# Two FNet-plus-attention layers on one core: the P·V sum's PSUM bank exchanged with the bank of the maxima, and six steps instead of eight between a tile's row maxima and its scores

## The chip, the core and the metric

The program runs on one NeuronCore of a Trainium2 chip. It uses the engines TensorE (PE in the profile; its weight loads stand apart as PEld), VectorE (DVE), ScalarE (ACT), GpSimd (POOL), and the queue engine SyncE (SP), which issues DMAs. The metric is the device time of one execution in microseconds. The kernel before took 3445.49 us in the median of three runs (3443.53 to 3445.89).

## What is computed

Two layers, one after the other. Each mixes x by a real Fourier transform over hidden size and sequence, and then adds multi-query attention with 32 heads of size 16 and one shared K and V:

```python
x = x + Re(DFT_seq(DFT_hidden(layernorm(x))))          # x: 2048 x 512
q = (layernorm(x) @ wq) -> 32 heads x 2048 x 16;  k, v = layernorm(x) @ wk, @ wv   # 2048 x 16 each
p = softmax(q @ k.T / 4)                                # 32 x 2048 x 2048
x = x + concat_heads(p @ v) @ wo
...                                                     # the same two again
```

## The kernel before

Each layer has a phase a (the two transforms, layer norm, K, V and Q, and some row maxima) and a phase b (the attention and the output projection). The change touches phase b alone, which the function `phase_b` writes out step by step.

Phase b walks over 16 tiles of 128 queries (index i), and each tile over 32 steps (s_); n = 32 i + s_ counts them through. A step takes half of the heads (hf 0 in steps 0 to 15, hf 1 in 16 to 31) against one chunk of 128 keys, and contains:

- **four scores** (`score`, L1119): K against four query pairs, 512 columns each, into a PSUM bank; ACT then takes the exponential of each bank into SBUF (L1121). Four banks `o.x` go round for this.
- **three maxima** of a later tile (`whole` with `max_of`, L450 and L451, and `part`, L1070 to L1075): query against 512 keys into a bank, and DVE reduces the bank to its maximum. `part` does two halves of 256 keys in one bank, with a one-element copy on DVE (L1072) between them. Three banks `o.banks` go round: a maximum takes the first of the list, and the bank goes to the end of the list.
- **the P·V matmuls** (`pv`, L1133) of the step two steps earlier, four matmuls in fp32 (eight records in the trace), summed over 16 steps into one bank "z". At the sum's end (pv of steps 15 and 31, so issued in steps 17 and 1) the bank is copied to SBUF, by ACT (L1144) or by DVE (L1142), and the next sum begins in the same bank one step later.

Step 17 also holds the output projection of the tile before (`o_proj`, 12 matmuls at L102 to L104 into one of the maxima's banks `po`, and ACT's copy of it, L1207).

How many maxima a step gets is decided by `share(n)`: three, or two where n % 32 == 1 and the maxima are at least SPARE (3) ahead of their due times. A step with two maxima gives the sum's end to DVE instead of ACT. The due times (`goals`) lie AHEAD steps before the end of a tile or half. When no maxima are left, n_max is 0, and the kernel changes to "wide" steps: exponentials of 1024 columns (L1114), in other banks.

The maxima of a tile reach its scores in this way, all of it placed by AHEAD = 8 (`at` is 24 for a whole tile): in steps at - 1 and at DVE reduces the partial maxima (`max_neg_a`, L594), in step at + 1 POOL splits them into a high and a low part (`max_neg_b`, L603 and L604), and in step at + 2 DVE transposes them (`max_rows`, L609) and 16 DMAs (L615), eight issued by SP and eight by POOL, write them into the rows 48, 49 and 112, 113 of the tile's queries `qT`. The first scores of the tile, in its step 0, read these rows. For tile 0's second half and for the halves of the tiles 14 and 15, the same goes on with half as many pairs, and for the second halves with `at` = 8.

Each engine works through its own list of instructions in order; a wait for a semaphore holds up everything behind it on that engine. The order in the lists is the order in which the code is written.

Of the kernel before, what the change touches and what calls it, by code (L numbers as in the profile page):

```python
# [22 lines left out]
NT = S // P  # L23
NK = D // P
TB = 4
NPAIR = H // 2
# [1 line left out]
KR = 64  # L28
M0 = 48
NSTEP = 32  # L30
AHEAD = 8
SPARE = 3


# [10 lines left out]
HALF = NPAIR // 2  # L45
# [3 lines left out]
def fnet_mqa_kernel(ctx: ExitStack, tc: tile.TileContext, x_in, ct, dt_, wq, wkv, wo, out):  # L49
    nc = tc.nc  # L50
# [160 lines left out]
    def make_layer(L, src, mid, dst, last):  # L211
        o = Layer()
# [232 lines left out]
            return o.mxp[i]  # L445

        def max_of(i, pr, g, c0, n, to):
            pm = (o.banks.pop(0) if o.banks else bank("y"))[:, :n]
            gs = slice(64 * g, 64 * g + KR)
            nc.tensor.matmul(pm, o.qT[i][gs, pr, :], kz[gs, c0:c0 + n], start=True, stop=True)  # L450
            nc.vector.reduce_max(to, pm, axis=AX.X)  # L451
            if o.banks:
                o.banks.append(pm)

        def max_two(pr, g, c0, to):
            pm = bank("y")
# [575 lines left out]
        ahead, parts = [], []  # L1032
# [62 lines left out]
        def done_with(i, pr):  # L1095
            return all(u[:2] > (i, pr) for u in todo + parts + ahead)

        ptiles = {}
        wide = []
# [26 lines left out]
        def pv(i, s_, n_max=3):  # L1126
            hf, c = divmod(s_, NT)
            if c == 0:
                acc[i, hf] = bank("z")
            a = acc[i, hf]  # L1130
            pt = ptiles.pop((i, s_))
            for j in range(4):
                nc.tensor.matmul(a[32 * j:32 * j + 32, :], v1[:, c, :], pt[:, j, :], start=c == 0, stop=c == NT - 1)  # L1133
            if c == NT - 1:
                oa = half(hf)
                if last and (i, hf) == (NT - 1, 1):
                    ob = half(0)[:, :256]
                    nc.scalar.copy(oa[:, :256], a[:, :256])
                    nc.vector.tensor_copy(ob, a[:, 256:])
                    oa = (oa, ob)  # L1140
                elif wide and hf == 0 or n_max == 2:
                    nc.vector.tensor_copy(oa, a)  # L1142
                else:
                    nc.scalar.copy(oa, a)  # L1144
                acc[i, hf] = oa
# [41 lines left out]
            nc.gpsimd.tensor_copy(bt["oh"][:, cs], bt["ot"][:, cs])  # L1187
            nc.gpsimd.tensor_sub(bt["ol"][:, cs], bt["ot"][:, cs], f(bt["oh"][:, cs]))

        def o_mm(k):  # L1190
            if k == 0:
                bt["po"] = o.banks.pop(0) if o.banks else bank("y")
            ks = slice(k * P, (k + 1) * P)
            mm3(bt["po"], bt["oh"][:, ks], bt["ol"][:, ks], woh[:, k, :], wol[:, k, :], k == 0, k == NK - 1)

# [2 lines left out]

        def o_proj(i):
            for k in range(NK):  # L1200
                o_mm(k)
            o_add(i)

        def o_add(i):
            if o.banks or wide:
                raw = half(3)
                nc.scalar.copy(raw, bt["po"])  # L1207
                o.banks.append(bt["po"])
                nc.gpsimd.tensor_add(bt["x"], raw, bt["x"])
            else:  # L1210
                nc.vector.tensor_add(bt["x"], bt["po"], bt["x"])
            (nc.sync if last else nc.gpsimd).dma_start(dst[i], bt["x"])
# [82 lines left out]
        def phase_b(nxt):  # L1295
            nonlocal woh, wol, osp
            o.x = pair() + pair()
            o.banks = [bank("y") for _ in range(3)]
            woh = slot(4, F32R).rearrange("p (k e) -> p k e", k=NK)
            wol = slot(5, F32R).rearrange("p (k e) -> p k e", k=NK)  # L1300
            def wo_load(j):
                st["wo", j] = half(4 + j)
                nc.sync.dma_start(st["wo", j], wo[:, j, :])

            behind = []
            for n in range(NT * NSTEP):
                i, s_ = divmod(n, NSTEP)
                n_max = share(n) if todo or parts or ahead else 0
                if len(behind) == 2:
                    pv(*behind.pop(0), n_max)  # L1310
                behind.append((i, s_))
                out_now = i > 0 and s_ == NT + 1
                if out_now:
                    o_proj(i - 1)
                if out_now and n_max == 3:
                    o.x.append(o.banks.pop())
                    o.banks.append(o.x.pop(0))
                if n_max == 0 and not wide:
                    banks_as(f"wide{L}")
                    o.banks = [bank("v")]  # L1320
                    wide.extend(bank("w") for _ in range(3))
                at = part_next() if n_max == 3 else None
                if at:
                    for k, v in zip("asMssMsb", (0, 1, 0, 3, 0, 1, 2, 1)):
                        if k == "s":
                            score(i, s_, v)
                        elif k == "M":
                            whole(v)
                        else:
                            part(at, v)  # L1330
                else:
                    g = side()
                    turns = ((g, 0), (1 - g, min(n_max, 2)), (2 + g, 0), (3 - g, n_max - 2))
                    if out_now and n_max == 2:
                        whole(g)
                        turns = ((1 - g, 0), (g, 1), (3 - g, 0), (2 + g, 0))
                    for j, m in turns:
                        score(i, s_, j)
                        for _ in range(m):
                            more_max()  # L1340
                if n in (1, 3):
                    q_half_store(12, 2 + n // 2)
                if i == 0 and 17 <= s_ <= 23 and s_ % 2:
                    q_half_store(14, s_ // 2 - 8)
                if 12 <= n < 16:
                    wo_load(n - 12)
                if n == 25:
                    osp = slot(3, F32R).rearrange("p (a h n) -> p a h n", a=2, h=2)
                if i == 0 and s_ in (16, 18, 20, 22):
                    j = s_ // 2 - 8  # L1350
                    nc.gpsimd.tensor_copy(woh[:, j, :], st["wo", j])
                    nc.gpsimd.tensor_sub(wol[:, j, :], st["wo", j], f(woh[:, j, :]))
                if i > 0:
                    for fn in out_tasks(i - 1).get(s_, ()):
                        fn()
                for j in range(2, NT):
                    if i == (j // 4 if j < 5 else j - 4 if j < 13 else j - 2):
                        at = {2: 0, 3: 12, 4: 6}.get(j, 0)
                        if s_ == at:
                            qT_load(j)  # L1360
                        if s_ == at + 4:
                            o.loaded.add(j)
                for fn in half_tasks(i).get(s_, ()):
                    fn()
                for at, j, p0, np_ in ((NT - AHEAD, i, HALF, HALF), (NSTEP - AHEAD, i + 1, 0, HALF if i >= NT - 3 else NPAIR)):
                    if j in (0, NT - 2, NT - 1) or j == i + 1 < NT:
                        for e in range(2):
                            if s_ == at - 1 + e:
                                assert done_with(j, p0 + np_ // 2 * (e + 1) - 1)
                                max_neg_a(j, p0, np_, parts=(e,))  # L1370
                        if s_ == at + 1:
                            max_neg_b(np_, nc.gpsimd)
                        if s_ == at + 2:
                            max_rows(j, p0, np_)
            if nxt is not None:
                wide.clear()
                banks_as(f"single{L + 1}")
                nxt.a_start()
            for at in behind:
                pv(*at)  # L1380
            if nxt is not None:
                o.banks = []
            return {**out_tasks(NT - 1), 12: [lambda: o_proj(NT - 1)]}
# [67 lines left out]
```

## Time and profile before

| | |
|---|---|
| median of three runs | 3445.49 us |
| the profiled execution's own time | 3445.71 us |
| its span, first to last instruction | 3443.9 us |
| what lies around the span | 1.8 us |
| granted TensorE clock | 0.999 |
| phase b of layer 0, first to last exponential | 621.9 to 1724.4 us |
| phase b of layer 1 | 2331.9 to 3433.9 us |
| one step of phase b | about 2.1 us |
| one wide step | about 1.85 us |

The busy time of PE comes from modelled ends of pipelined matmuls, so 99% does not mean that PE is at its peak. Groups of instructions carry the line that recorded them, so L1133 is every P·V matmul.

### The profile page before, as it was taken

What the parts mean: (1) busy time and instruction counts of PE and PEld (TensorE: products, weight loads), DVE (VectorE), ACT (ScalarE), POOL (GpSimd) and SP (SyncE); (2) the same over time, 40 slices, a digit from 0 to 9 for tenths busy, and PEclk for the clock granted to TensorE, in tenths of its full rate; (3) what the DMA queues carried; (4) which work ended last, traced back from release to release, by engine and by line L of the source; (5) the groups of instructions that cost most, each with busy time, mean ns of one, the idle gap of its engine ahead of it and who ended that gap; (6) DMA issues with size and microseconds to landing.
All of it is one profiled execution on the core that took longest, in us unless ns stands there. A gap on an engine that the chain in (4) does not pass through costs nothing.

```text
span 3443.9 us, 68599 instructions
## 1 busy us (share of the span) xinstructions
PE 3415.1 (99%) x25532; PEld 2016.1 (59%) x25532; DVE 2664.0 (77%) x5792; ACT 2665.6 (77%) x5228; POOL 936.9 (27%) x1478
## 2 busy tenths in 40 slices
PE   8999999999999999999999999999999999999999
PEld 6888979544444444444378989894444444444443
DVE  6264766899999999999432747669989998999893
ACT  4234644899999999999932256549999999999998
POOL 4255453312222222222313354522111111111111
PEclk9999999999999999999999999999999999999999
DMA  6445252321111100111143352523111111011110
GB/s 189 149 157 190 75 169 81 88 65 34 39 36 51 36 27 24 51 36 27 42 141 116 127 171 102 153 72 91 48 39 36 51 36 39 23 37 38 33 29 26
DMA packets 225554, 255.88 MB, mean 74 GB/s; under 512 B 52896, under 2 KB 175040, under 8 KB 218052
## 3 DMA queue, kind: packets, MB, share of 16 engines
q1 hardware_dynamic: 210932, 234.04, 21.8%
q0 software_dynamic: 14144, 17.33, 1.6%
q8 instruction: 201, 3.29, 0.4%
q14 instruction: 133, 1.09, 0.1%
q10 hardware_dynamic: 144, 0.13, 0.0%
HBM read 187.69 MB, written 65.79 MB: 74 GB/s over the span
## 4 chain that ended last, share of the span: by engine, by line
PE 92%; issue 3%; DVE 2%; ACT 2%; POOL 1%; DMA 1%; SPq 0%; DVEq 0%; ACTq 0%; POOLq 0%
PE z L1133 30%; PE x L893 11%; PE x L1119 7%; PE x L1070 6%; PE y L1119 5%; PE x L450 5%; PE y L1070 4%; PE y L450 3%; PE y L541 3%; PE x L102 3%; PE x L104 3%; PE x L103 2%; PE y L102 2%; PE y L103 2%; PE y L104 2%
## 5 line engine op out<-in xcount | busy, mean ns | idle before, releaser
L1121 ACT ACTIVATE slot<-x 128x512 f32<-128x512 f32 x2212 | 1189.0, 604 | 17.4 <-PE x L1119 2.6
L1133 PE MATMUL z<-slot,v 128*32 128x512 f32 x8192 | 1102.1, 605 | 0.8
L1121 ACT ACTIVATE slot<-y 128x512 f32<-128x512 f32 x1692 | 927.8, 606 | 8.6
L451 DVE TENSOR_REDUCE mxp<-x 128x1 f32<-128x512 f32 x1126 | 739.7, 685 | 29.7
L451 DVE TENSOR_REDUCE mxp<-y 128x1 f32<-128x512 f32 x830 | 549.2, 685 | 26.2 <-PE y L450 2.8
L1119 PE MATMUL x<-slot,kz 64*128 64x512 f32 x1662 | 516.1, 423 | 0.7 <-DMA slot<-craw 0.7
L1119 PE MATMUL y<-slot,kz 64*128 64x512 f32 x1218 | 415.3, 430 | 0.0
L1075 DVE TENSOR_REDUCE mxp<-x 128x2 f32<-128x512 f32 x556 | 378.8, 681 | 1.0 <-PE y L1119 1.0
L1070 PEld LDWEIGHTS x<-kz,slot 64*128 64x128 f32 x844 | 154.8, 183 | 348.9 <-DVE mxp L451 342.1
L893 PE MATMUL x<-cl,xnh 64*128 64x512 f32 (+1 forms) x1536 | 358.6, 354 | 0.0
L893 PE MATMUL x<-ch,xnl 64*128 64x512 f32 (+1 forms) x1536 | 346.4, 358 | 3.3 <-ACT xnl L652 3.3
L893 PE MATMUL x<-ch,xnh 64*128 64x512 f32 (+1 forms) x1536 | 346.9, 358 | 0.2
L450 PE MATMUL x<-kz,slot 64*128 64x512 f32 x858 | 343.9, 415 | 0.0
L1133 PEld LDWEIGHTS z<-slot,v 128*32 128x32 f32 x8192 | 167.1, 108 | 229.4 <-issue 184.4
L1070 PE MATMUL x<-kz,slot 64*128 64x256 f32 x844 | 280.2, 332 | 0.0
L1075 DVE TENSOR_REDUCE mxp<-y 128x2 f32<-128x512 f32 x400 | 272.5, 681 | 0.0
L1119 PEld LDWEIGHTS x<-slot,kz 64*128 64x128 f32 x1662 | 262.3, 185 | 13.6 <-ACT slot L1121 7.8
L1070 PEld LDWEIGHTS y<-kz,slot 64*128 64x128 f32 x564 | 103.7, 184 | 233.1 <-DVE mxp L451 219.8
L450 PE MATMUL y<-kz,slot 64*128 64x512 f32 x582 | 236.6, 418 | 0.6 <-DVE mxp L451 0.4
L893 PEld LDWEIGHTS x<-ch,xnh 64*128 64x128 f32 x1536 | 215.3, 184 | 17.2 <-issue 5.2
L893 PEld LDWEIGHTS x<-ch,xnl 64*128 64x128 f32 x1536 | 213.3, 184 | 19.8 <-issue 6.1
L893 PEld LDWEIGHTS x<-cl,xnh 64*128 64x128 f32 x1536 | 217.1, 185 | 8.9
(270 smaller groups left out, 6792.5 us busy)
## 6 DMA issues: line engine op xcount, KB each, us to landing
craw<-ct_in SPq DMA_DIRECT2D x112, 512.0 KB
slot<-qd SPq DMA_DIRECT2D x44, 1024.0 KB
qd<-row SPq DMA_DIRECT2D x144, 128.0 KB
od<-row SPq DMA_DIRECT2D x252, 64.0 KB
row<-wqd SPq DMA_DIRECT2D x48, 256.0 KB
row<-x_in SPq DMA_DIRECT2D x32, 256.0 KB
mid<-row POOLq DMA_DIRECT2D x32, 256.0 KB, 2.4
craw<-ct_in SPq DMA_DIRECT2D x32, 256.0 KB
```

Of the source, the lines that this page charges most:

```text
L102: nc.tensor.matmul(ps_, ah, bh, start=start, stop=False)
L103: nc.tensor.matmul(ps_, ah, bl, start=False, stop=False)
L104: nc.tensor.matmul(ps_, al, bh, start=False, stop=stop)
L450: nc.tensor.matmul(pm, o.qT[i][gs, pr, :], kz[gs, c0:c0 + n], start=True, stop=True)
L451: nc.vector.reduce_max(to, pm, axis=AX.X)
L541: nc.tensor.matmul(pm, o.qT[i][gs, pr, :], k[gs, c0:c0 + 512], start=True, stop=True)
L893: nc.tensor.matmul(z[d], a[gs, s, d * P:(d + 1) * P], b[gs, :], start=first and q < 2 and e == 0, stop=last and q > 1 and e == len(turns) - 1)
L1070: nc.tensor.matmul(pm[:, 256 * g:256 * g + 256], o.qT[i][gs, pr, :], kz[gs, c0:c0 + 256], start=True, stop=True)
L1075: nc.vector.reduce_max(partial(i)[:, pr, :, k], pm.rearrange("p (a n) -> p a n", a=2), axis=AX.X)
L1119: nc.tensor.matmul(e, kz[64 * g:64 * g + KR, c * P:(c + 1) * P], o.qT[i][64 * g:64 * g + KR, cp:cp + 4, :], start=True, stop=True)
L1121: nc.scalar.activation(ptiles[i, s_][:, j, :], e, AF.Exp, scale=DH ** -0.5)
L1133: nc.tensor.matmul(a[32 * j:32 * j + 32, :], v1[:, c, :], pt[:, j, :], start=c == 0, stop=c == NT - 1)
```

## The change

AHEAD goes from 8 to 6. `share(n)`, `left` and `goals` are as they were, so the later due times let the steps n = 353, 385, 417, 449 and 481 of each layer have two maxima as well: 15 such steps in a layer, where there were ten (33, 65, ... 321). The five sums that end there are copied by DVE instead of ACT. The five maxima that these steps leave out come later, and the first wide step is n = 489, where it was 488.

The P·V sums get a named bank `o.z`. Where DVE copies a sum's end (tiles 0 to 13), the next sum begins in the bank that a maximum has used last, and the copied bank goes to the end of the maxima's list. After an output projection, the next sum takes the projection's bank, and the sum's old bank goes to the maxima. The earlier exchange in step 17, of the projection's bank with a bank of the scores, is gone. Around tiles 14 and 15 the rules bring the sum back into its first bank before the wide steps.

The block with the maxima's last steps (L1365 to L1374) now stands ahead of the output tasks, the loads of queries and the half tasks of a step, instead of behind them.

```diff
-AHEAD = 8
+AHEAD = 6
...
         def max_of(i, pr, g, c0, n, to):
-            pm = (o.banks.pop(0) if o.banks else bank("y"))[:, :n]
+            b = o.banks.pop(0) if o.banks else bank("y")
+            pm = b[:, :n]
...
             if o.banks:
-                o.banks.append(pm)
+                o.banks.append(b)
...
         def pv(i, s_, n_max=3):
             hf, c = divmod(s_, NT)
             if c == 0:
-                acc[i, hf] = bank("z")
+                acc[i, hf] = o.z
...
                 elif wide and hf == 0 or n_max == 2:
                     nc.vector.tensor_copy(oa, a)
+                    if not wide and i < NT - 2:
+                        o.z = o.banks.pop()
+                        o.banks.append(a)
                 else:
                     nc.scalar.copy(oa, a)
...
-        def o_mm(k):
+        def o_mm(k, i=0):
             if k == 0:
-                bt["po"] = o.banks.pop(0) if o.banks else bank("y")
+                bt["po"] = o.banks.pop(next((k for k, b in enumerate(o.banks) if i == NT - 2 and b is o.zb), 0)) if o.banks else bank("y")
...
         def o_add(i):
             if o.banks or wide:
                 raw = half(3)
                 nc.scalar.copy(raw, bt["po"])
-                o.banks.append(bt["po"])
+                if not wide and o.z is not bt["po"] and (i < NT - 3 or bt["po"] is o.zb):
+                    o.banks.append(o.z)
+                    o.z = bt["po"]
+                else:
+                    o.banks.append(bt["po"])
...
             o.banks = [bank("y") for _ in range(3)]
+            o.z = o.zb = bank("z")
...
                 if out_now:
                     o_proj(i - 1)
-                if out_now and n_max == 3:
-                    o.x.append(o.banks.pop())
-                    o.banks.append(o.x.pop(0))
...
+                for at, j, p0, np_ in ((NT - AHEAD, i, HALF, HALF), (NSTEP - AHEAD, i + 1, 0, HALF if i >= NT - 3 else NPAIR)):
+                    ...
+                        if s_ == at + 1:
+                            max_neg_b(np_, nc.gpsimd)
+                        if s_ == at + 2:
+                            max_rows(j, p0, np_)
                 if i > 0:
                     for fn in out_tasks(i - 1).get(s_, ()):
                         fn()
...
                 for fn in half_tasks(i).get(s_, ()):
                     fn()
-                for at, j, p0, np_ in ((NT - AHEAD, i, HALF, HALF), ...
```

**DVE, near the end of tile 5 of layer 0.** The rows are DVE's list before; `nm` and `ms` are the maxima on their way, `mxp` the partial maxima of later tiles, and each L1075 is the last maximum of a step. The transposition L609 stands in step 26, one step ahead of the layer norm's L1268 in step 27.

```order
L1258 BN_AGGR mv<-mt 128x2
L1072 COPY x<-x 1x1
L451 TENSOR_REDUCE mxp_10992<-x 128x1
L451 TENSOR_REDUCE mxp_10992<-y 128x1
L1075 TENSOR_REDUCE mxp_10992<-x 128x2
L609 STREAM_TRANSPOSE mt<-ms 128x64
L1072 COPY x<-x 1x1
L451 TENSOR_REDUCE mxp_11905<-y 128x1
L451 TENSOR_REDUCE mxp_11905<-x 128x1
L1075 TENSOR_REDUCE mxp_11905<-x 128x2
L1268 TENSOR_SCALAR lnv<-mv 128x1
L1269 TENSOR_SCALAR lnw<-lnv 128x1
```

The same list of the changed kernel, whose lines are numbered a little higher (L610 is the transposition, L1076 a step's last maximum, L1276 and L1277 the layer norm's).

```order
L595 TENSOR_REDUCE nm<-mxp_9817 128x16
L1073 COPY y<-y 1x1
L452 TENSOR_REDUCE mxp_11896<-y 128x1 x2
L1076 TENSOR_REDUCE mxp_11896<-y 128x2
L1276 TENSOR_SCALAR lnv<-mv 128x1
L1277 TENSOR_SCALAR lnw<-lnv 128x1
L1073 COPY y<-y 1x1
L452 TENSOR_REDUCE mxp_11896<-y 128x1 x2
L1076 TENSOR_REDUCE mxp_11896<-y 128x2
L610 STREAM_TRANSPOSE mt<-ms 128x64
L1279 TENSOR_SCALAR rs<-lnw 128x1
```

The transposition has moved behind two more steps' maxima, into step 28.

**POOL, near the end of tile 3 of layer 0.** Before, POOL splits the maxima, issues its eight DMAs, and then scales the attention output of the first half (L1181 to L1188):

```order
L603 CAST ms<-nm 128x2x16
L604 TENSOR_TENSOR ms<-nm,ms 128x2x16
L615 DMA xnl<-mt 1x16x32 x8
L440 MEMSET mxp_10992 128x32x2
L1181 TENSOR_TENSOR row_10887<-row_10887,row_10888 128x256
L1187 CAST slot_8594<-row_10887 128x256
L1188 TENSOR_TENSOR slot_8594<-row_10887,slot_8594 128x256
L1273 TENSOR_TENSOR lnw<-rs 128x1
```

In the changed kernel (L1185 to L1192 scale, L616 are the DMAs, L1281 begins the layer norm's short operations):

```order
L604 CAST ms<-nm 128x2x16
L605 TENSOR_TENSOR ms<-nm,ms 128x2x16
L1185 TENSOR_TENSOR row_10880<-row_10880,row_10881 128x256
L1191 CAST slot_8590<-row_10880 128x256
L1192 TENSOR_TENSOR slot_8590<-row_10880,slot_8590 128x256
L616 DMA xnl<-mt 1x16x32 x8
L1281 TENSOR_TENSOR lnw<-rs 128x1
```

The three scaling operations have come between the split and the eight DMAs.

**PE, from the end of step 0 to step 2 of tile 4**, with the semaphores that each waits for. Before, the new sum's first P·V matmul (step 2) goes into the bank that DVE copies in step 1, and waits for DVE; the maximum behind it waits for nothing:

```order
L1133 MATMUL z<-slot_11096,v_75 32x512 x4
L1119 MATMUL x<-xnl,kz 128x512 [waits Activation_49]
L1119 MATMUL y<-xnl,kz 128x512 [waits Activation_49]
L450 MATMUL x<-kz,slot_10345 128x512 [waits DVE_49] x2
L1119 MATMUL y<-xnl,kz 128x512 [waits Activation_49] x2
L1133 MATMUL z<-slot_11118,v_75 32x512 [waits DVE_49]
L1133 MATMUL z<-slot_11118,v_75 32x512 x3
L1070 MATMUL x<-kz,slot_10345 128x256
```

In the changed kernel (L1134 is P·V, L1120 a score, L451 and L1071 maxima):

```order
L1134 MATMUL z<-slot_11089,v_75 32x512 x4
L1120 MATMUL x<-xnl,kz 128x512 [waits Activation_49] x2
L451 MATMUL y<-kz,slot_10340 128x512 [waits DVE_49] x2
L1120 MATMUL x<-xnl,kz 128x512 [waits Activation_49] x2
L1134 MATMUL y<-slot_11111,v_75 32x512 [waits DVE_49]
L1134 MATMUL y<-slot_11111,v_75 32x512 x3
L1071 MATMUL z<-kz,slot_10340 128x256 [waits DVE_49]
```

The new sum goes into a bank y, and its wait for DVE is for the last maximum of step 0, which stands ahead of the copy in DVE's list; the wait for the copy of z is now that of the maximum behind the P·V matmuls.

More of the change, by code (lines that the diff above doesn't have):

```diff
@@ L1200, in o_proj @@
             for k in range(NK):
-                o_mm(k)
+                o_mm(k, i + 1)
             o_add(i)
@@ L1314, in phase_b @@
                     o_proj(i - 1)
-                if out_now and n_max == 3:
-                    o.x.append(o.banks.pop())
-                    o.banks.append(o.x.pop(0))
                 if n_max == 0 and not wide:
+                    assert o.z is o.zb
                     banks_as(f"wide{L}")
@@ L1352, in phase_b @@
                     nc.gpsimd.tensor_sub(wol[:, j, :], st["wo", j], f(woh[:, j, :]))
+                for at, j, p0, np_ in ((NT - AHEAD, i, HALF, HALF), (NSTEP - AHEAD, i + 1, 0, HALF if i >= NT - 3 else NPAIR)):
+                    if j in (0, NT - 2, NT - 1) or j == i + 1 < NT:
+                        for e in range(2):
+                            if s_ == at - 1 + e:
+                                assert done_with(j, p0 + np_ // 2 * (e + 1) - 1)
+                                max_neg_a(j, p0, np_, parts=(e,))
+                        if s_ == at + 1:
+                            max_neg_b(np_, nc.gpsimd)
+                        if s_ == at + 2:
+                            max_rows(j, p0, np_)
                 if i > 0:
@@ L1364, in phase_b @@
                     fn()
[L1365 to L1374, printed above, removed]
             if nxt is not None:
```

## The prediction, made before the changed kernel was run

> **What bounds the kernel now.** I read the busy times of the page first, then one tile of phase b in the windows, then the chain of waits.
>
> ```profile
> PE 3415.1 (99%) x25532; PEld 2016.1 (59%) x25532; DVE 2664.0 (77%) x5792; ACT 2665.6 (77%) x5228; POOL 936.9 (27%) x1478
> core 0: us, PE busy (x) PEld busy (x) DVE busy (x) ACT busy (x) POOL busy (x), PEclk, DMA share, GB/s
> 1035.90:1105.20 69.30, 69.25 (x525) 31.47 (x523) 64.43 (x141) 66.55 (x131) 16.26 (x35) 1.00 0.14 41
> ```
>
> The second pair is the stretch of tile 6 in layer 0. In 69.30 us PE is busy 69.25, ACT 66.55 and DVE 64.43: three engines work side by side and none has more than 5 us to spare, most of it in one place. POOL has 53 us to spare. The next rows, from the chain of waits in tile 1, show that place. Each is the P·V group of one step, so the distance of two rows is the length of a step.
>
> ```profile
> 723.19 0.99 PE z L1133 x8
> ...
> 728.30 1.06 PE z L1133 x8
> ...
> 730.37 1.01 PE z L1133 x8
> ...
> 732.53 0.99 PE z L1133 x8
> ```
>
> Steps last 5.11, 2.07 and 2.16 us. The long one holds the output projection, in which PE does other work for some 3 us and ACT and DVE run dry. The two steps after it are not shorter than the others. So **a pause of one engine in phase b is not caught up later**; it goes into the time in full. That reading carries most of what follows.
>
> **The change part by part.** The sum is made against the profiled execution's own 3445.7 us, 0.2 us above the median of the runs.
>
> *Five more steps with two maxima in a layer.* The kernel before has tiles of both kinds, and the transposition L609, once in each tile, measures them.
>
> ```profile
> L609 DVE STREAM_TRANSPOSE mt<-ms x10: 232/233/235, 748.3 to 1371.8; 128x64 f32<-128x64 f32 x10
> L609 DVE STREAM_TRANSPOSE mt<-ms x4: 199/232/234, 1371.8 to 1580.5; 128x64 f32<-128x64 f32 x3, 128x32 f32<-128x32 f32 x1
> L609 DVE STREAM_TRANSPOSE mt<-ms x10: 232/234/236, 2458.4 to 3081.3; 128x64 f32<-128x64 f32 x10
> L609 DVE STREAM_TRANSPOSE mt<-ms x4: 201/234/235, 3081.3 to 3289.8; 128x64 f32<-128x64 f32 x3, 128x32 f32<-128x32 f32 x1
> 1677.37 16.61 ACT L1114 ACTIVATE slot<-w 128x1024 f32<-128x1024 f32 x18
> ```
>
> In layer 0 nine tiles with such a step took 623.5 us, 69.28 each, and three without it 208.7, or 69.57. In layer 1 it is 69.21 and 69.50. The difference is 0.29, and ten tiles get it: **-2.9 us**. The maxima left out come at the end, where one more ordinary step replaces a wide one. A wide step has two activations of 1024 columns, 2 x 16.61/18 = 1.85 us; an ordinary one takes 2.09 (half of 4.17, below). That is +0.24 in each layer, **+0.5 us**.
>
> *The new sum no longer waits for DVE's copy.* In the answer for line L1133, the weight load that opens a P·V group sat idle as in the first two rows (us in all, times); the other two rows are from the answer for the scores, L1119, and serve below.
>
> ```profile
>   issue: 184.4, 794
>   DVE row L1142: 7.0, 20
>   ACT row L1207: 7.3, 28
>   DMA slot<-craw: 1.8, 4
> ```
>
> Twenty sums waited 0.35 us for the copy, where the ordinary pause is 0.23. After the change the bank is free already, since its last reduction stands ahead of the copy on DVE; the maximum that now waits for the copy comes a whole P·V group later, which covers it. If that cover went, the same 0.1 would come back. Gain 0.12 in each of 14 tiles and two layers, **-3.4 us**; its bounds are 0 (ACT may be the next to be late) and 28 x 0.35 = -9.8.
>
> *The scores no longer use the projection's bank.* By the third row above, 28 times a score waited 0.26 us for ACT's copy of the projection. What is late next is ACT:
>
> ```profile
> 1004.28 0.59 ACT L1207 COPY row<-x 128x512 f32<-128x512 f32 x1 [2.03 <-issue]
> 1004.77 1.09 ACT L1121 ACTIVATE slot<-y 128x512 f32<-128x512 f32 x2
> 1005.73 1.11 ACT L1121 ACTIVATE slot<-x 128x512 f32<-128x512 f32 x2
> 1006.87 1.08 ACT L1121 ACTIVATE slot<-y 128x512 f32<-128x512 f32 x2
> ```
>
> From that copy on, ACT goes from one activation to the next without a gap, so an earlier score finds it busy. I take **0**; bounds 0 and -7.3. The next sum waits for the projection's copy instead of its own; that ends at 1004.87, and the next P·V group comes only after the step's seven matmuls.
>
> *Six steps instead of eight.* This is the large term. Rows from the timeline at the end of tile 5, the two last of them from the first step of tile 6:
>
> ```profile
> 1024.78 0.68 DVE L1075 TENSOR_REDUCE mxp<-x 128x2 f32<-128x512 f32 x1
> 1025.38 0.23 DVE L609 STREAM_TRANSPOSE mt<-ms 128x64 f32<-128x64 f32 x1
> 1028.95 0.67 DVE L1075 TENSOR_REDUCE mxp<-y 128x2 f32<-128x512 f32 x1
> 1025.64 5.00 SPq L615 DMA_DIRECT2D slot<-mt  x8
> 1034.44 0.34 SPq L582 DMA_DIRECT2D slot<-qd  x1
> 1025.90 3.88 POOL L615 DMA_DIRECT2D slot<-mt  x8 [3.81 <-DVE x L1072]
> 1029.79 0.75 POOL L1181 TENSOR_TENSOR row<-row,row 128x256 f32<-128x256 f32 x1
> 1035.36 0.38 PE L1070 MATMUL x<-kz,xnl 64*128 64x256 f32 x1
> 1035.36 0.50 PE L1119 MATMUL y<-slot,kz 64*128 64x512 f32 x1
> ```
>
> The transposition follows the last maximum of step 26 (1024.78); after the change it follows that of step 28 (1028.95), 4.17 us later. SP then issues its eight DMAs one after the other, 5.00 us, so its last is issued at about 1030.05. When does that one land?
>
> ```profile
> L615 SPq DMA_DIRECT2D slot<-mt x8: 567/586/601, 1025.6 to 1030.0; - x8
> L615 POOL DMA_DIRECT2D slot<-mt x8: 484/484/516, 1025.9 to 1029.3; - x8
> DMA to landing us min/median/max: 1.5/1.6/1.6
> 1017.38 0.34 SPq L1169 DMA_DIRECT2D rd<-dc  x1
> 1019.14 0.57 SPq L1177 DMA_DIRECT2D row<-rd  x1
> SPq L1177 <- DMA rd<-dc: 34.7, 60, 2.4
> ```
>
> The profile gives 1.6 us for the DMAs that POOL issues. For SP's it gives none, but L1177 waits for the landing of L1169, and came 1.76 us after its issue. With 1.76 the last of SP's DMAs landed at 1031.81, and the scores of tile 6 began at 1035.36, 3.55 later. So the wait did not show. **Moved by 4.17, it lands at 1035.98, 0.62 us after the scores are due**. POOL's last lands about 0.9 earlier (1029.3 + 1.6), so SP's decides. The first score of a step 0 works on the upper 64 partitions and needs SP's eighth DMA, whose rows lie there. It stands second in the step: behind it on PE stand all other matmuls of the step, and ACT and DVE wait for those. Nothing covers it, and by the long step above it isn't caught up.
>
> There are 17 such places in a layer, the boundaries into the tiles 1 to 15 and the second halves of the tiles 0 and 14; the second half of tile 15 lies among wide steps, where DVE runs ahead. With 1.6 a place costs 0.46, with 1.5 it costs 0.36; an SP run like the next row adds 0.85.
>
> ```profile
> 1233.51 5.85 SPq L615 DMA_DIRECT2D xnl<-mt  x8
> ```
>
> At seven of these 34 places SP's run took over 5.5 us instead of the usual 5.0 to 5.4, some 0.6 more on the mean; I add 4.4 us for them. So 34 x 0.62 = 21.1, with 4.4 **+25.5 us**; bounds 34 x 0.36 = 12 and, with every run like the last row, 34 x 1.47 = 50.
>
> On the other queues: on POOL the scaling (L1181 and two more, some 2 us) now stands ahead of the eight DMAs. It can start when the split is done, two steps before the transposition, and is over in time. The layer norm's short POOL work begins later, but POOL is idle for most of the tile. On SP the load L582 at 1034.44 is pushed by some 0.4 (5.00 + 4.17 after 1025.64 is 1034.81); it fetches the queries of a later tile, and nobody is near needing them.
>
> Sum: 3445.7 - 2.9 + 0.5 - 3.4 + 0 + 25.5 = **3465.4 us**.
>
> **The rivals.**
>
> *SP's writes land in time (not slower).* The mechanism is the time from issue to landing on SP's queue; the point from which it decides is 1035.36 - 4.17 - 1030.05 = 1.14 us. If SP's DMAs land faster than that, no place costs anything, and the time is 3445.7 - 5.8 = 3439.9, within 0.2%. For it: no row shows the landing of exactly these DMAs. Against it: 1.5 as the least of POOL's landings, and 1.76 for L1169. The Trainium skill, "DMA: Bandwidth & Descriptors", section "Latency and other measured facts", has the first byte after about 0.6 us for DMAs of the sync queue and 1 us for those of GpSimd; by that, SP's would land 0.4 before POOL's, after an estimated 1.2 us, and the 34 places would cost only 0.06 each, for some 3442 us. The 1.76 us of L1169 doesn't bear that out. The same page's section "Anatomy of one DMA — SWDGE (gpsimd) path" gives about 2.0 us of fixed cost for any DMA; the trace has 1.6 there, and with 2.0 each place would cost 0.24 more, an estimated 3473.6 us.
>
> *The wait comes, but half of it is caught up.* ACT has a few hundredths of idle time in many steps and DVE too. If they and PE made up half of each wait, the term would be 12.8 us, and the time 3452.7; with the usual runs at every place, 10.5 and 3450.4. The steps after the projection speak against it.
>
> *The start after the wait costs more.* The score has eight DMAs to wait for, and what PE needs to go on after such a wait no tile shows. The nearest row is the fourth of those above: four times in all, in the first tiles, scores waited for DMAs, 0.45 us each. If that much came on top, a place would cost 1.07, the term would be 36.4 + 4.4, and the time 3480.7.
>
> **How the numbers follow.** The forecast, 3455 to 3476 with 3465 as its centre, gets 0.65; writes in time 0.12 (of which 0.05 with the larger gain of the banks, so faster by over 0.2%); half caught up 0.13, of which 0.10 lie below 3452.4; the dearer start 0.10. A measurement of this kernel can tell about 0.2%, 6.9 us, from no change. So slower 0.65 + 0.10 + 0.03 = 0.78, same 0.07 + 0.10 = 0.17, faster 0.05. The range from 3447 to 3477 holds the forecast and most of the half-caught case, and leaves out the writes in time and most of the dearer start.
>
> **What would show it.** In the profile after: PE's scores (L1120) waiting for the DMAs into qT, some 30 times and 0.6 us each; tiles of about 69.7 to 70.0 us by the distance of the transpositions, all 14 of a layer alike; no P·V group waiting for DVE's copy; 30 copies of sums on DVE; a first wide step one step later. I am wrong if the waits for these DMAs are missing, or if they are there and the distance of the transpositions stays under 69.3.

## The result, and the profile after

The changed kernel takes **3495.8 us** in the median of four runs (3494.0 to 3499.7). The kernel before took 3445.7 in the four runs beside it (3443.5 to 3446.9). The ratio is 1.0148, with a 95% interval from 1.0135 to 1.0160: slower by 50 us. The forecast was 3465, with a range up to 3477. The direction held, the size did not.

The profiled execution is the longest of the four: 3499.7 us, span 3497.9, granted clock 0.996. It is 54.0 us above the profiled execution before, and 4 above its own median. First the busy times of the page, then the answer for the DMAs of the maxima, whose line is now L616 (the lines below the first edit are one to eight higher than before).

```profile
PE 3431.8 (98%) x25524; PEld 2011.8 (58%) x25524; DVE 2669.9 (76%) x5794; ACT 2661.3 (76%) x5222; POOL 934.5 (27%) x1478
who waited for it (us, times):
  PE x L1120: 34.1, 28
DMA to landing us min/median/max: 1.5/1.6/4.8
```

DVE and ACT have nearly the same work as before. What is new is in the third row: 28 scores waited for these DMAs, 34.1 us in all. That is 1.2 us each, not 0.6. And one of POOL's DMAs took 4.8 us to land, where 1.6 was the most before.

The answers for DVE's copy of a sum (who waited for it) and for the P·V group (its idle time until) have these rows:

```profile
  PEld y L1134: 8.0, 28
```

```profile
  issue: 201.0, 841
```

The transposition, once in each tile, with the times of its first and last start:

```profile
L610 DVE STREAM_TRANSPOSE mt<-ms x10: 222/223/224, 754.8 to 1391.1; 128x64 f32<-128x64 f32 x10
L610 DVE STREAM_TRANSPOSE mt<-ms x4: 190/222/223, 1391.1 to 1601.7; 128x64 f32<-128x64 f32 x3, 128x32 f32<-128x32 f32 x1
L610 DVE STREAM_TRANSPOSE mt<-ms x9: 234/235/236, 2493.2 to 3060.8; 128x64 f32<-128x64 f32 x9
L610 DVE STREAM_TRANSPOSE mt<-ms x4: 234/234/235, 3060.8 to 3273.8; 128x64 f32<-128x64 f32 x4
```

The distances are 70.70 and 70.20 in layer 0 and 70.95 and 71.00 in layer 1, against 69.2 to 69.6 before. So a tile costs 0.6 to 1.8 us more, and not all tiles alike. A mean hides single places: of the eight tiles behind the 70.95 one took 76.4 (2493.2 to 2569.6) and the other seven 70.2 on the mean, and the tile just ahead of these rows, from 2417.0 to 2493.2, took 76.2. Two boundaries show why. The first is an ordinary one, from the timeline at the end of tile 4 of layer 0:

```profile
965.66 0.22 DVE L610 STREAM_TRANSPOSE mt<-ms 128x64 f32<-128x64 f32 x1
965.91 5.00 SPq L616 DMA_DIRECT2D slot<-mt  x8
966.18 3.88 POOL L616 DMA_DIRECT2D slot<-mt  x8 [1.97 <-DVE y L1073]
971.48 0.38 PE L1071 MATMUL y<-kz,xnh 64*128 64x256 f32 x1
972.30 0.47 PE L1120 MATMUL x<-slot,kz 64*128 64x512 f32 x1 [0.44 <-DMA slot<-mt]
```

Before the change the maximum and the score that open a tile began together (both at 1035.36 in the prediction's rows). Now the score begins 0.82 later. SP's eighth DMA is issued at 970.32 and lands at 972.06, by the completions in the trace, so 1.74 after its issue; the forecast had 1.76. From the landing to the score it is another 0.24. The second is a bad one, the end of tile 0 in layer 1:

```profile
2417.03 0.23 DVE L610 STREAM_TRANSPOSE mt<-ms 128x64 f32<-128x64 f32 x1
2417.33 5.06 SPq L616 DMA_DIRECT2D slot<-mt  x8
2417.44 0.73 POOL L1185 TENSOR_TENSOR row<-row,row 128x256 f32<-128x256 f32 x1 [3.69 <-DMA row<-rd]
2419.40 3.91 POOL L616 DMA_DIRECT2D slot<-mt  x8
2422.75 0.34 SPq L583 DMA_DIRECT2D slot<-qd  x1
2427.76 0.76 PE L1120 MATMUL x<-slot,kz 64*128 64x512 f32 x1 [4.51 <-DMA slot<-mt]
2428.32 0.66 PE L1120 MATMUL x<-slot,kz 64*128 64x512 f32 x2
2429.52 1.94 PE L1134 MATMUL z<-slot,v 128*32 128x512 f32 x8
```

POOL's eight DMAs stand behind the scaling L1185, and that waits for a load until 2417.44. So POOL begins 2.1 us after SP, and its eighth DMA goes out at 2422.82, just behind SP's load of the next queries (L583, 1 MB) at 2422.75. The chain of waits has what follows:

```profile
2419.95 2.87 POOL slot L616 x6
2422.82 4.85 DMA slot<-mt
2427.67 0.09 issue
```

Landed after 4.85 instead of 1.6 us, this write keeps PE idle for 4.51 us. And when PE goes on it is slower: a P·V group takes 1.94 where 1.06 is usual. The windows behind four such pauses have the granted clock in the column after POOL:

```profile
972.30:976.50 4.20, 4.20 (x31) 1.74 (x33) 3.66 (x6) 3.66 (x8) 3.69 (x7) 1.00 0.74 262
1043.59:1047.79 4.20, 4.20 (x21) 1.67 (x21) 2.61 (x4) 2.12 (x5) 3.92 (x3) 0.59 0.70 250
2427.76:2431.96 4.20, 4.20 (x17) 1.95 (x19) 2.36 (x4) 2.06 (x4) 0.00 (x0) 0.50 0.02 4
2577.59:2581.79 4.20, 4.20 (x31) 1.73 (x33) 3.67 (x6) 3.66 (x8) 0.00 (x0) 1.00 0.66 248
```

They follow pauses of 0.44, 1.57, 4.51 and 1.81 us. Behind two of them the clock is about half of full speed for some 4 us. It fell in this way at four of the 34 places, and cost about 1.5 us each, in the steps behind the pause.

**Where the 54 us are.** The two executions can be laid side by side step by step, by the start of each step's first exponential. The 34 places and the one or two steps behind each hold 54.6 us. Tile 0 has 2.5 more in its step 23 (below), step 26 of layer 0 is 0.2 longer in each tile (2.5 together), the change to wide steps costs 1.6. Against that, the five new two-maximum steps of each layer save 3.4 and the banks 3.5; tile 0's step 1 is 1.1 shorter in the two layers together, a difference of granted clock that comes up again below. The sum is 53; the last 1 us is not split.

### The profile page after: what moved, and what is told of

Same layout as the page of the kernel before. It is cut to its first block, busy times and chain, and to the rows that moved or that the text cites. A ratio compares the mean times of both kernels' runs of the same rounds, so it can differ in the third digit from the quotient of the medians.

```text
span 3497.9 us, 68613 instructions
## 1 busy us (share of the span) xinstructions
PE 3431.8 (98%) x25524; PEld 2011.8 (58%) x25524; DVE 2669.9 (76%) x5794; ACT 2661.3 (76%) x5222; POOL 934.5 (27%) x1478
## 4 chain that ended last, share of the span: by engine, by line
PE 84%; issue 4%; SPq 3%; ACT 2%; DMA 2%; DVE 2%; POOL 2%; DVEq 0%; ACTq 0%; POOLq 0%
PE z L1134 13%; PE y L1134 13%; PE x L1120 12%; PE x L894 11%; PE y L1071 7%; PE y L451 6%; SPq L616 3%; PE y L542 3%; PE x L102 2%; PE x L104 2%; PE x L103 2%; PE y L102 2%; PE y L103 2%; PE y L104 2%; PE z L1071 1%
## 5 line engine op out<-in xcount | busy, mean ns | idle before, releaser
L1122 ACT ACTIVATE slot<-x 128x512 f32<-128x512 f32 x3912 | 1999.7, 605 | 82.0 <-PE y L451 47.2
L452 DVE TENSOR_REDUCE mxp<-y 128x1 f32<-128x512 f32 x1684 | 1095.9, 685 | 92.7 <-PE y L451 50.3
L1120 PE MATMUL x<-slot,kz 64*128 64x512 f32 x2888 | 799.7, 428 | 30.3 <-DMA slot<-mt 28.0
L1134 PE MATMUL z<-slot,v 128*32 128x512 f32 x4608 | 627.2, 608 | 0.0
L1076 DVE TENSOR_REDUCE mxp<-y 128x2 f32<-128x512 f32 x808 | 551.3, 682 | 0.0
L1071 PEld LDWEIGHTS y<-kz,slot 64*128 64x128 f32 x1188 | 218.1, 184 | 493.3 <-DVE mxp L452 477.0
L451 PE MATMUL y<-kz,slot 64*128 64x512 f32 x1236 | 491.5, 418 | 0.6 <-DVE mxp L452 0.4
L1134 PE MATMUL y<-slot,v 128*32 128x512 f32 x3584 | 477.7, 605 | 0.0
L1120 PEld LDWEIGHTS x<-slot,kz 64*128 64x128 f32 x2888 | 428.0, 185 | 66.3 <-ACT slot L1122 39.8
L1071 PE MATMUL y<-kz,slot 64*128 64x256 f32 x1188 | 393.9, 332 | 2.1 <-DVE y L1073 1.8
L451 PEld LDWEIGHTS y<-kz,slot 64*128 64x128 f32 x1236 | 224.7, 185 | 60.5 <-DVE y L1073 14.6
L1185 POOL TENSOR_TENSOR row<-row,row 128x256 f32<-128x256 f32 x63 | 46.0, 730 | 583.4 <-DMA row<-rd 561.9
L452 DVE TENSOR_REDUCE mxp<-z 128x1 f32<-128x512 f32 x280 | 192.2, 686 | 12.4 <-PE z L451 2.3
L542 PE MATMUL y<-kz,slot 64*128 64x512 f32 x488 | 189.3, 397 | 2.8 <-DVE mxe L558 2.2
```

The costliest lines, as they stand in the source:

```text
L542: nc.tensor.matmul(pm, o.qT[i][gs, pr, :], k[gs, c0:c0 + 512], start=True, stop=True)
L1071: nc.tensor.matmul(pm[:, 256 * g:256 * g + 256], o.qT[i][gs, pr, :], kz[gs, c0:c0 + 256], start=True, stop=True)
L1076: nc.vector.reduce_max(partial(i)[:, pr, :, k], pm.rearrange("p (a n) -> p a n", a=2), axis=AX.X)
L1120: nc.tensor.matmul(e, kz[64 * g:64 * g + KR, c * P:(c + 1) * P], o.qT[i][64 * g:64 * g + KR, cp:cp + 4, :], start=True, stop=True)
L1122: nc.scalar.activation(ptiles[i, s_][:, j, :], e, AF.Exp, scale=DH ** -0.5)
```

## The experiments

All of them were compared with runs of the kernel before on the same chip. The theories: **W**, the time is the wait of a tile's first scores for the last landing of the maxima's DMAs; **X**, the exchange of banks or the new order of the code costs a good part; later **Q**, a DMA issued behind the 1 MB load queues behind it.

| kernel | median, us | against before's own runs | ratio, 95% interval |
|---|---|---|---|
| changed kernel | 3495.8 | +50.1 | 1.0135 to 1.0160 |
| AHEAD = 8 | 3441.9 | -3.0 | 0.9984 to 1.0001 |
| AHEAD = 7, SPARE = 1 | 3448.7 | +3.8 | 1.0003 to 1.0021 |
| before with AHEAD = 6 | 3569.7 | +124.9 | 1.0351 to 1.0379 |
| eight DMAs | 3447.9 | +3.0 | 1.0000 to 1.0019 |
| late load | 3491.0 | +46.3 | 1.0116 to 1.0147 |
| block behind | 3571.6 | +126.9 | 1.0353 to 1.0381 |
| late load, SP 7 and POOL 9 | 3485.8 | +41.1 | 1.0106 to 1.0134 |
| eight DMAs, late load | 3441.7 | -3.0 | 0.9983 to 1.0000 |
| AHEAD = 8, SPARE = 0 | 3440.3 | -3.7 | 0.9981 to 0.9998 |
| eight DMAs, late load, AHEAD = 8, SPARE = 0 | 3440.0 | -4.1 | 0.9979 to 0.9997 |
| eight DMAs, late load, AHEAD = 5 | 3492.6 | +48.6 | 1.0125 to 1.0156 |

**The banks and the order alone.**

```diff
-AHEAD = 6
+AHEAD = 8
```

> The changed kernel with AHEAD back at 8: the bank exchange and the new place of the block alone, ten two-maximum steps in a layer as before. Theory W (all of the added 50 us are waits of step 0 for the maxima's DMAs): nothing waits, so 3445 to 3447, within 0.1% of the kernel before; the steps at the sums' ends only trade a tenth with their neighbours. Rival X (the exchange of banks or the new order costs what the forecast missed, some 30 us): 3465 to 3480. Rival G (the exchange gains 3.4 us, as forecast): 3442.

Measured 3441.9. The time is that of rival G, the gain of the banks, though the interval just reaches no change (1.0001); what shows the gain is the steps. The tiles 1 to 14 are 0.11 us shorter in layer 0 and 0.15 in layer 1, 3.5 in all: step 17 loses 0.19 and step 18 gives 0.14 of it back. The change to wide steps is 0.4 to 0.7 longer in each layer. Step 1 of tile 0 is 1.2 shorter in both layers, as in most of the later kernels, though in the changed kernel in one only. The windows of that step show a different granted clock: 0.60 and 0.59 in the two layers of the kernel before, 1.00 in both here, 1.00 and 0.55 in the changed kernel. Why, no run here shows, and whether the new banks or the new order have a part in it stays open. Of the 5.3 us between the two profiled executions 2.5 are this step, and some of the 3.0 in the medians may be. So none of the 50 us added comes from the banks, or from the new order with AHEAD = 8.

**One step of delay, not two.**

```diff
-AHEAD = 6
-SPARE = 3
+AHEAD = 7
+SPARE = 1
```

> The changed kernel with AHEAD = 7 and SPARE = 1, which keeps all 15 two-maximum steps in a layer: the transposition comes one step later than before, not two. Theory W: SP's last DMA lands 6.2 us after the transposition (7.3 in the slow SP runs), the first score is due 9.7 - 2.1 = 7.6 us after it, so hardly a place waits: 3440 to 3444. Rival L (each step of delay costs the same, half of the 50 us): 3465 to 3472.

Measured 3448.7. The waits are gone as W has it, but for one boundary of layer 1, which cost 2.6 and 1.7 in the step behind it. So delay isn't priced by the step, and rival L falls. The time is still 5 us above what I expected: in layer 0 the steps 26 and 28 became 0.2 longer each, in nearly every tile, and in layer 1 they did not; probably the reductions and the transposition of the maxima meet the layer norm's work on DVE there, which no run tests by itself; and in tile 0 step 23 costs 1.1 and 0.9. The timelines of tile 0, of the changed kernel and of the kernel before, show that one:

```profile
669.26 1.32 SPq L1166 DMA_DIRECT2D dc<-od  x2
671.97 0.25 DVE L1170 RECIPROCAL dc<-dc 128x16 f32<-128x16 f32 x1 [1.03 <-DMA dc<-od]
```

```profile
666.77 1.32 SPq L1162 DMA_DIRECT2D dc<-od  x2
670.72 0.24 DVE L1166 RECIPROCAL dc<-dc 128x16 f32<-128x16 f32 x1
```

SP's queue is busy in tile 0. With its eight DMAs two steps later, the loads of `dc` behind them go out 2.5 us later than before, and DVE waits 1.03 us for one.

**The delay without the change.** This is the kernel before with AHEAD = 6 alone.

> The kernel before with AHEAD = 6 alone: its own banks, and the block behind the half tasks. Theory W: the same waits as in the changed kernel, so 3490 to 3500; the split on POOL now stands behind the scaling in step 27, which can only make the transposition later, so rather the upper end or above. Rival X (the banks or the order cost 30 us): 3465 to 3470.

Measured 3569.7, which no theory had: 74 us above the changed kernel. So the order does matter here, in the other direction: the new place of the block saves much once AHEAD is 6. The next kernel isolates it.

**The block behind again.**

```diff
-                for at, j, p0, np_ in ((NT - AHEAD, i, HALF, HALF), ...
-                    ...
                 if i > 0:
                     for fn in out_tasks(i - 1).get(s_, ()):
...
                 for fn in half_tasks(i).get(s_, ()):
                     fn()
+                for at, j, p0, np_ in ((NT - AHEAD, i, HALF, HALF), ...
+                    ...
```

> The changed kernel with the block of the maxima's last steps put back behind the output tasks, the loads and the half tasks. Theory Q: POOL's eight DMAs then stand behind the layer norm's short work on POOL and go out after SP's 1 MB load, above all in layer 0 where POOL has that work in the same step: as slow as the kernel before with AHEAD = 6, less the 3 us of the banks: 3562 to 3570. Rival X2 (the 74 us between that kernel and the changed one come from the banks): 3490 to 3500.

Measured 3571.6, a little above the range. The new banks are in this kernel and the time is still that of the kernel before with AHEAD = 6, so the 74 us are the place of the block. From the timeline of this kernel, at the end of tile 3 of layer 0:

```profile
910.15 0.22 DVE L610 STREAM_TRANSPOSE mt<-ms 128x64 f32<-128x64 f32 x1
910.40 5.00 SPq L616 DMA_DIRECT2D xnl<-mt  x8
913.31 0.19 POOL L1284 TENSOR_TENSOR rs<-rs,lnw 128x1 f32<-128x1 f32 x1
913.79 3.92 POOL L616 DMA_DIRECT2D xnl<-mt  x8 [0.30 <-DVE mxp L452]
915.76 0.34 SPq L583 DMA_DIRECT2D xnh<-qd  x1
921.62 0.76 PE L1120 MATMUL x<-xnl,kz 64*128 64x512 f32 x1 [5.31 <-DMA xnl<-mt]
```

POOL first works off the twelve short instructions of the layer norm (the last is L1284) and issues its DMAs 3.4 us after SP. Half of them go out behind the 1 MB load L583 of 915.76, and PE idles 5.31 us. Nearly every tile of layer 0 is like that. Layer 1, where the layer norm is not on POOL in these steps, loses 0.6 to 0.8 at six of its 15 boundaries and over 2.1 at one only. The granted clock of the whole span is 0.985.

**Eight DMAs in place of sixteen.**

```diff
             for a in range(4):
                 for g in range(2):
-                    for r in range(2):
-                        row = 64 * g + M0 + r
-                        b, c = divmod(n * (2 * g + r), 32)
-                        (nc.gpsimd if r else nc.sync).dma_start(
-                            f(o.qT[i][row:row + 1, p0:p0 + n, 32 * a:32 * a + 32]),
-                            mt[32 * a + c:32 * a + c + n, 32 * b:32 * b + 32])
+                    row = 64 * g + M0
+                    b, c = divmod(2 * n * g, 32)
+                    (nc.gpsimd if g else nc.sync).dma_start(
+                        f(o.qT[i][row:row + 2, p0:p0 + n, 32 * a:32 * a + 32]),
+                        mt[32 * a + c:32 * a + c + 2 * n, 32 * b:32 * b + 32])
```

> The changed kernel (AHEAD = 6) with eight DMAs of 32 runs in place of 16 of 16 runs: each carries the high and the low row of one half and one quarter of the queries, four issued by SP, four by POOL. Theory W: SP's last is issued 1.9 us after the transposition and lands at about 3.6, two us ahead of the scores (due at 5.6), so the waits go and all 15 two-maximum steps stay: 3439 to 3443. Rival S (the wait is not for the last landing but a dearer start of the scores that follow the transposition by six steps): no change, 3490 to 3500. If each DMA with twice the runs takes twice as long to issue, it stays near 3495 as well, and the SP rows would show it.

Measured 3447.9, 5 above the range of W, but 47 of the 50 us are gone, with AHEAD = 6 and all 15 two-maximum steps kept. Rival S falls, and this is the strongest evidence for W: the steps, the banks and the arithmetic are those of the changed kernel; the DMAs are fewer, and the last lands earlier. Most of what is left above 3443 is one boundary, at the end of tile 10 in layer 0, where POOL's fourth DMA went out behind the 1 MB load: 4.65 us and 1.26 in the step behind.

**The load two steps later.**

```diff
-                        at = {2: 0, 3: 12, 4: 6}.get(j, 0)
+                        at = {2: 0, 3: 12, 4: 6}.get(j, 2)
```

> The changed kernel with one number altered: the 1 MB load of a later tile's queries is issued by SP in step 2 of a tile, not in step 0, so two steps after the maxima's DMAs. Theory Q (in layer 1, at the ends of tiles 0 and 1, POOL's last DMA was issued after that load and landed 4.4 us after its issue, not 1.6, because it queued behind the load): these two places lose their excess, some 13 us of the profiled 54: 3480 to 3486. Rival P (POOL's own queue was slow there, the load is a bystander): 3493 to 3500.

Measured 3491.0, 4.8 less than the changed kernel (3.8 by the column of differences); the profiled span fell by 6.8. Q is right about the mechanism, and I was wrong about its share. The same boundary as above:

```profile
2416.75 0.24 DVE L610 STREAM_TRANSPOSE mt<-ms 128x64 f32<-128x64 f32 x1
2419.02 3.90 POOL L616 DMA_DIRECT2D slot<-mt  x8
2424.11 0.47 PE L1120 MATMUL x<-slot,kz 64*128 64x512 f32 x1 [1.16 <-DMA slot<-mt]
```

POOL is as late as before, still held by the scaling, but its eighth write now lands in the usual time: 7.0 us after the transposition, not 10.4. The two bad boundaries together fell from 14.5 to 7.2 us with the steps behind them. The rest is POOL's late start itself and the lower clock behind it (0.71 and 0.59 in the windows).

The same edit on the eight-DMA kernel:

> The kernel with eight DMAs of 32 runs, and the query load in step 2. Theory Q: its one bad boundary (end of tile 10 in layer 0, 5.9 us with the step behind it) was POOL's last DMA behind the load; it goes: 3440 to 3443, faster than the kernel before by 0.05 to 0.15%. Rival P: unchanged, 3446 to 3450.

Measured 3441.7, 6 us less than without it, as Q has it. The bad boundary fell from 5.9 to 1.3 us.

**One DMA from SP to POOL.**

```diff
-                        (nc.gpsimd if r else nc.sync).dma_start(
+                        (nc.gpsimd if r or a == 3 and g else nc.sync).dma_start(
```

> As the kernel with the late load, and one of SP's eight DMAs given to POOL (seven on SP, nine on POOL). Theory W: SP's last lands 0.6 earlier, at 5.6 us after the transposition, POOL's last at 5.7 where it was 5.25, so the first score begins 0.45 earlier at each of 34 places, 15 us less than the kernel with the late load alone: 3465 to 3471. Rival S (what the scores wait for is not the last landing): no difference from that kernel, within 3 us.

Measured 3485.8, only 5.2 less. At the quiet places the cost fell from between 0.6 and 1.0 to mostly 0.3 to 0.6, about as W has it. But POOL, now with the longer run, was late at some places, and three of them took most of it back: they cost 7.7, 3.9 and 3.1 us. The worst, the second half of tile 0 in layer 1:

```profile
2376.76 2.52 POOL L616 DMA_DIRECT2D slot<-mt  x5 [4.07 <-PE y L1071]
2381.17 0.44 SPq L583 DMA_DIRECT2D xnh<-qd  x1
2381.91 1.99 POOL L616 DMA_DIRECT2D slot<-mt  x4 [2.63 <-issue]
2389.27 0.76 PE L1120 MATMUL x<-slot,kz 64*128 64x512 f32 x1 [7.08 <-DMA qd<-slot]
```

Between its fifth and its sixth DMA POOL stood still for 2.63 us, for nothing that the profile shows, and the last four then went out behind other transfers, the 1 MB load L583 first among them. The profile names a write of SP for the last wait (qd<-slot); by the completions POOL's last write landed at 2388.97, and PE's wait for its semaphore ended at 2389.00. Such pauses occur in the changed kernel too (2.60 at the end of tile 1 in layer 1).

**W as a rule, at another landing time.** The kernel with eight DMAs and the late load, with AHEAD = 5:

> Eight DMAs of 32 runs, the query load in step 2, AHEAD = 5: the transposition one step later than in the changed kernel. Theory W as a rule for any number of DMAs (a place costs landing plus 0.25 us, less the time at which the score is due): the score is due 5.6 - 2.1 = 3.5 us after the transposition, the last DMA lands 4.1 after it, so 0.85 at each of 34 places, 29 us over the same kernel with AHEAD = 6 (3441.7): 3465 to 3478. Rival (with half the DMAs the wait no longer decides): 3440 to 3445. Where single waits go over 1.3 us and TensorE's granted clock drops behind them, up to 10 us more.

Measured 3492.6, above the range. Layer 1 follows the rule: 15.5 us at 17 places, eight of them at 0.6 to 0.7. Layer 0 took 36, 1.7 to 1.9 at a quiet place, and at five places the clock fell too. Its timeline at the end of tile 2:

```profile
825.90 0.23 DVE L610 STREAM_TRANSPOSE mt<-ms 128x64 f32<-128x64 f32 x1
827.01 0.19 POOL L1283 TENSOR_TENSOR rs<-rs,lnw 128x1 f32<-128x1 f32 x1
827.61 2.46 POOL L615 DMA_DIRECT2D xnh<-mt  x4 [0.41 <-DVE mxp L452]
831.59 0.46 PE L1119 MATMUL x<-xnh,kz 64*128 64x512 f32 x1 [1.63 <-DMA xnh<-mt]
```

The transposition is now in step 29 and the layer norm's short work, in step 28, stands ahead of POOL's DMAs after all. The last lands at 831.18, 5.05 after the transposition; by the rule the place costs 5.05 + 0.25 - 3.5 = 1.8. So the rule holds at such a place, with POOL's landing in place of SP's, and I had again overlooked what stands ahead on POOL. It leaves out the lower clock.

**Keeping the gains.** Two kernels with the transposition in its old step and SPARE = 0, which gives thirteen two-maximum steps: one with sixteen DMAs, one with eight.

```diff
-AHEAD = 6
-SPARE = 3
+AHEAD = 8
+SPARE = 0
```

> The changed kernel with AHEAD = 8 and SPARE = 0: bank exchange, no later transposition, and thirteen two-maximum steps in a layer. Against the kernel with AHEAD = 8 alone (3441.9) three more such steps in each layer, 0.34 us each as the tiles 11 to 15 of the changed kernel show: 3439 to 3441. Rival (the slack used up makes the maxima late, or the wide steps start later for as much): 3441 to 3445.

> Eight DMAs of 32 runs, the query load in step 2, AHEAD = 8, SPARE = 0 (thirteen two-maximum steps). Nothing waits for the DMAs even with sixteen, so the same time as the kernel with thirteen two-maximum steps and sixteen DMAs, 3439 to 3441; if the freed queues are worth something by themselves, up to 3 us less.

Measured 3440.3 and 3440.0, both as expected and both below the kernel before, by 0.11 and 0.12% (upper ends of the intervals 0.9998 and 0.9997). Part of that may be the clock of tile 0's step 1 again, which is 1.00 in both layers of both profiled executions. The DMAs make no difference once nobody waits for them. The first is the change without its delay, two numbers away from it.

## Why the prediction was wrong, point by point

- **A pause in phase b is not caught up.** It held, and more than that: at four of the 34 places a pause cost more than its length, because of the lower clock behind it.
- **Five more two-maximum steps, -2.9.** It held: 0.34 for each in the tiles 11 to 15, 3.4 in all. With AHEAD = 8 three of them in a layer saved 2.1 us by the steps in the tiles 11 to 13, of which the tiles 14 and 15 gave 1.1 back; in the medians it is 0.8, taken against before's own runs.
- **One step for a wide one, +0.5.** Too small by 1.1. The change to wide steps costs 0.4 to 0.7 more in each layer even where no step is moved (AHEAD = 8), so this belongs to the new bank rules.
- **The new sum's bank, -3.4.** The size held: 3.5 by the steps; the 3.0 in the medians may in part be the clock of tile 0's step 1. The sign in the profile that I named did not, by the rows of the result: 28 P·V groups still stand as waiting for DVE's copy, 0.29 us each. That is hardly more than their ordinary pause of 0.24; mostly the copy ends 0.02 us before such a group begins, which is probably why the profile names it.
- **The scores and the projection's bank, 0.** Not tested by itself. The gain of both edits together is no larger than the term above, so it may stand.
- **Six steps instead of eight, +25.5.** This is the step that failed: it measured 54.6. Its first half was right. SP's last DMA lands 1.74 us after its issue, and the quiet place waits for it. Three sentences of the term were wrong. "Nothing covers it" took the price of a wait for its length alone: 0.24 us from the landing to the score came on top, so 0.82 for a quiet place, 27.9 at 34 places where I had 21.1. At four places the lower clock came on top, about 6. The third rival, with 0.45 for such a start, had the idea, but no clock in it. "POOL's last lands about 0.9 earlier, so SP's decides" and "the scaling ... is over in time" failed at two places, which cost 9.4 by the later landing alone. I had counted the 1 MB load as one that nobody is near needing, and so it is; but it is what a late write queues behind. The rest is SP's long runs, 6.7 where I had 4.4, the halves of tiles 0 and 14 (1.0 to 1.3 each, 1.4 together over the 0.82), and some 3 us that I could not split.
- **Not in the forecast at all:** 2.5 us in tile 0, whose SP queue is full, and 2.5 in step 26 of layer 0, where DVE's reductions of the maxima meet other work.
- **What would show it.** The 30 copies of sums on DVE are there (32 with those of the wide steps), and so is the later wide step. The waits came 28 times, but 1.2 us each, and the distances are 70.2 to 71.0, not 69.7 to 70.0, and not alike.

The bounds of the term, 12 to 50, were nearly wide enough. The range left out their upper part, because I gave the dearer start only 0.10 and no case at all to a late POOL.

## What to carry to other kernels

When the lead of a small DMA is shortened, its margin has to cover the worst landing and not the usual one: every queue that carries a part of it counts, with what stands ahead on that engine and which large transfer is issued around the same time. A stall of the engine that bounds the kernel is priced at its length plus its restart, and a spell of lower clock can come on top. Before shortening a lead, make the transfer itself shorter: eight DMAs instead of sixteen took back 47 of 50 us here.

## What the runs showed of the hardware that I had not expected

- The granted clock of TensorE fell for some 4 us behind pauses as short as 1.57 us in the changed kernel (0.59 in the window behind it) and 1.15 us in the one with the late load (0.71), but not behind one of 1.81, so the length alone doesn't decide it. The Trainium skill, "TensorE: Matmul & The Clock Gate", section "Why this matters for your kernels", advises against idle gaps above some 3 us; in these kernels half of that or less was enough.
- A write of POOL's queue, issued 0.07 us after a 1 MB load of SP's queue, landed 4.85 us after its issue, where 1.6 is usual. The last completions of the write and of the load stand at 2427.67 and 2427.83, so the write came through only as the load ended. The Trainium skill, "DMA: Bandwidth & Descriptors", section "Queues, rings and completion order", has each DMA engine take turns between its queues, packet by packet; no completion of the write is seen here before the load was nearly through.
- A DMA of 32 short runs took SP about as long to issue as one of 16: 2.68 us for four, against 5.00 for eight. It landed a little later, 1.9 us against 1.6 in the median of POOL's.
- POOL's queue stood still for some 2.6 us now and then between two DMAs, and some of SP's issues took 0.7 to 1.1 us more than the usual 0.6. Why, no run here shows.
